# Transform and dense layers on one core: the dense layers read tokens in the order in which the transform's last stage makes them

## The chip, the cores and the metric

The kernel runs on one core of a Trainium2 chip. The metric is the device time of one execution in microseconds. The core has a matrix engine (TensorE, PE in the profile, its weight loads PEld), a vector engine (VectorE, DVE), an activation engine (ScalarE, ACT), GpSimd (POOL) and SyncE (SP), which here only issues transfers. Each takes its instructions strictly in order; they wait for each other by semaphores.

## The reference

```python
# x: (8, 3008, 256); filters: (1505, 256); w_in: (256, 2048); w_out: (2048, 256)
X = np.fft.rfft(x, axis=1)
Y = X * (filt_r + 1j * filt_i)[None]
y = np.fft.irfft(Y, n=3008, axis=1)           # 8 sequences, filtered along the tokens
h = y.reshape(24064, 256) @ w_in
g = 0.5 * h * (1.0 + erf(h / sqrt(2)))
out = g @ w_out                               # (24064, 256), float32
```

## The kernel before

Two things share TensorE: a Fourier transform with its inverse, per batch (8 batches of 3008 tokens), and two dense layers, per tile of 512 tokens (47 tiles, in the order of the tokens).

**Transform.** 3008 = 47 x 64 is split into two factors, and each direction into two stages. For batches 1 to 7 these are `s1` (L382), then a write to DRAM (`R1`) and a read back in another layout (`r1`, L413, tile `b_sb`); `s2` (L420), two matmuls and one product with the filter on VectorE (tile `p`); `s3` (L431, its second half is evacuated by `s3_out`, L448), after each group of four s2; a write to DRAM (`R2`) and a read back (`r2`, L457, tile `d_sb`); and `s4` (L465). Batch 0 goes another way, without DRAM (`c1` to `c4`), ahead of everything else.

A token of a batch has the number 32 m + w, with m from 0 to 93 and w from 0 to 31. An `s4` unit makes, for one half of the 256 channels, four values of w for all m: 376 tokens, four neighbours in every 32. Eight groups (u = 0 to 7) of two halves make a batch. They are written to `ring` (tile `y_sb`), which holds two batches with channels on the partitions, at the place of their token number:

```python
yv = self.ring[:, half, o:o + self.S].rearrange("c (m w) -> c m w", w=HB)[:, :, 4 * grp:4 * grp + 4]
```

So the first dense tile of a batch needs all sixteen units. Half 1 is evacuated by ScalarE, half 0 by VectorE (in batch 1 from group 4 on by ScalarE too).

**Dense layers.** `mm1` (L577) makes 128 of 2048 hidden values for 512 tokens, two matmuls of 512 columns, and ScalarE's gelu stores them as `g_sb`. `mm2_seven` (L643) makes the second layer of the tile before with seven instead of eight block products, so VectorE first makes sums of blocks (`sums_1` to `sums_3`, L621 to L641) and afterwards combines results (L674 to L688) in `ost`. A tile's two stores of 256 rows each, which are whole rows of the output, are issued by SyncE (L690).

**Order.** The program is written out by hand in slots, 16 per tile. A slot has what `put(slot, ...)` entered in it, in the order of the calls, then 7 matmuls of 128 columns of `mm2_seven`, then one `mm1`. Batch b is transformed while the tiles of batch b - 1 go through the dense layers; `first(b)` is the slot of the first tile with tokens of b. In the loop over batches, `s1` and `n1` are first slot and spacing of the four s1, `r1` the slot of their read-back, `s2`, `n2` and `group` first slot, spacing and length of a group of the twelve s2, `r2` the slot of the read-backs, `s4` and `n4` first slot and spacing of the sixteen s4 units. For batches 3 to 7 these sixteen stand in sixteen slots one after the other, from 17 ahead of `first(b)`.

**Buffers.** PSUM has 3 banks `h` for `mm1` (and one tile of each s1 and s3), 2 banks `o` for `mm2_seven`, and 3 banks `f` for the stages s1 to s4. `d_sb`, which holds two groups, has 3 buffers. Tile 5 (`late`) holds the last tokens of batch 0 and the first of batch 1; its `mm1` start six slots late and then go faster.

Of the kernel before, what the change touches and what calls it, by code (L numbers as in the profile page):

```python
# [20 lines left out]
HB = 32  # L21
RND = 12582912.0
TCH = 512
TURNS = 64.0


def _dram(src, off, dims):
    return dataclasses.replace(src, offset=src.offset + off, ap=[list(d) for d in dims])


class _Mix:
# [433 lines left out]
    def s4(self, b, grp, half):  # L465
        nc = self.nc
        o = b % 2 * self.S
        d = self.st[b, "d", grp // 2]
        ps = self.bank("ps_s4")
        for i in range(4):  # L470
            nc.tensor.matmul(ps[:, 94 * i:94 * i + 94],  # L471
                             lhsT=d[:, (grp % 2) * 4 + i, 128 * half:128 * half + 128],
                             rhs=self.T4a[:, 4 * grp + i], start=True, stop=True)
        yv = self.ring[:, half, o:o + self.S].rearrange("c (m w) -> c m w", w=HB)[:, :, 4 * grp:4 * grp + 4]
        pv = ps[:, 0:376].rearrange("c (i m) -> c m i", i=4)
        self._evac(yv, pv, "act" if half or b == 1 and grp > 3 else False, 1.0 / self.S)

# [75 lines left out]
    def c4(self, u, eng):  # L553

        if u == 0:

            self.ring = self.py.tile([128, 2, 2 * self.S], BF16, tag="y", name="y_sb")
        d = self.st[0, "d", u // 2]
        for half in range(2):
            ps = self.bank("ps_c4", "h" if (2 * u + half) % 5 < 3 else "o")  # L560
            for i in range(4):
                self.nc.tensor.matmul(ps[:, 94 * i:94 * i + 94],
                                      lhsT=d[:, 4 * (u % 2) + i, 128 * half:128 * half + 128],
                                      rhs=self.T4c.rearrange("p a b -> p (a b)"), start=True, stop=True)
            yv = self.ring[:, half, 0:self.S].rearrange("c (m w) -> c m w", w=HB)[:, :, 4 * u:4 * u + 4]
            self._evac(yv, ps[:, 0:376].rearrange("c (i m) -> c m i", i=4), eng[half], 1.0 / self.S)


# [22 lines left out]
    def mm2(self, t, s):  # L591
        nc = self.nc
        tile_i, q = s // 4, s % 4
        g = self.st["g", t]
        if s % 8 == 0:
            self.st["o"] = self.bank("ps_o", "o").rearrange("p (a b) -> p a b", a=2)
        ps = self.st["o"]
        for i in range(4):
            jc = 4 * q + i
            nc.tensor.matmul(ps[:, tile_i % 2, :], lhsT=g[:, jc, tile_i * 128:tile_i * 128 + 128],  # L600
                             rhs=self.w_out_sb[:, jc, :], start=(jc == 0), stop=(jc == 15))
        if s % 8 == 7:
            ost = self.po.tile([128, 2, 256], FP32, tag="ost", name="ost")
            nc.vector.tensor_copy(out=ost, in_=ps)
            r0 = t * TCH + (tile_i - 1) * 128
            nc.sync.dma_start(out=self.out[r0:r0 + 256, :].rearrange("(s p) o -> p s o", p=128), in_=ost)

    def weight_sums(self):

# [33 lines left out]
    def mm2_seven(self, t, lo, hi):  # L643

        nc, v = self.nc, self.nc.vector.tensor_tensor
        a11, a12, s2, a22 = self.quarters(t)
        w = self.w_out_sb.rearrange("p (i k) (n o) -> p k n i o", k=2, n=2)
        q = self.w_sums
        s31, s4 = self.st["s", t], self.st.get(("s4", t))
        ops = ((a11, w[:, 0, 0]), (a12, w[:, 1, 0]), (s2, q[:, 1]), (s31[:, :, 0], q[:, 2]),  # L650
               (s31[:, :, 1], q[:, 0]), (a22, q[:, 3]), (s4, w[:, 1, 1]))
        last = t == self.B * self.S // TCH - 1
        for n in range(lo, hi):
            m, sub, i = n // 16, n // 8 % 2, n % 8
# [4 lines left out]
            nc.tensor.matmul(ps[:, (m + 1) % 2, sub, :], lhsT=a[:, i, 128 * sub:128 * sub + 128], rhs=b[:, i],  # L659
                             start=i == 0, stop=i == 7)  # L660
# [12 lines left out]
            if m == 0:  # L673
                nc.vector.tensor_copy(out=t1, in_=p1)  # L674
            elif m == 2:
                v(out=c(0, 0), in0=t1, in1=p0, op=ALU.add)  # L676
                if last:
                    self.store(t, 0, 0, nc.sync)
                v(out=t1, in0=t1, in1=p1, op=ALU.add)
            elif m == 4:  # L680
                v(out=t3, in0=t1, in1=p0, op=ALU.subtract)  # L681
                v(out=c(1, 1), in0=t3, in1=p1, op=ALU.add)
                if last:
                    self.store(t, 1, 1, nc.scalar)
                v(out=t1, in0=t1, in1=p1, op=ALU.add)
            else:
                for h, tt, p in ((1, t3, p0), (0, t1, p1)):
                    v(out=c(h, 1 - h), in0=tt, in1=p, op=ALU.add)  # L688
                    r0 = t * TCH + 256 * h
                    nc.sync.dma_start(out=self.out[r0:r0 + 256, :].rearrange("(s p) o -> p s o", p=128),  # L690
                                      in_=self.st["c"][h])

    def store(self, t, h, k, eng):
        r0, k = t * TCH + 256 * h, slice(128 * k, 128 * k + 128)
        eng.dma_start(out=self.out[r0:r0 + 256, k].rearrange("(s p) o -> p s o", p=128), in_=self.st["c"][h][:, :, k])

    def finish(self, t, m, sub, ps):

        h = 6 - m
        c, tt = self.st["c"][h], self.st["t"][:, h]  # L700
        k = slice(128 * (1 - h), 128 * (1 - h) + 128)
        self.nc.vector.tensor_tensor(out=c[:, sub, k], in0=tt[:, sub], in1=ps[:, (m + 1) % 2, sub], op=ALU.add)
        if h == 1:
            if sub == 1:
                self.store(t, 1, 0, self.nc.sync)
            return
        r0 = t * TCH + 128 * sub
        (self.nc.sync if sub else self.nc.scalar).dma_start(out=self.out[r0:r0 + 128, k], in_=c[:, sub, k])


@with_exitstack
def kernel(
# [9 lines left out]
    m = _Mix(ctx, tc, x, filt_r, filt_i, moe_w_in, moe_w_out, out)  # L722
# [115 lines left out]
    def put(slot, f, *a):  # L838
        at.setdefault(slot, []).append((f, a))

    def first(b):
        return (b * S // TCH) * 16

    for b in range(1, B):
        hi = first(b)
        if b == 1:
            s1, n1, r1, s2, n2, group, r2, s4, n4 = 0, 3, 12, 27, 2.5, 12, 64, 73, 0.75
        elif b == 2:
            s1, n1, r1, s2, n2, group, r2, s4, n4 = hi - 92, 3.7, hi - 78, hi - 70, 3.4, 14, hi - 24, hi - 17, 1
        else:  # L850
            s1, n1, r1, s2, n2, group, r2, s4, n4 = hi - 94, 3.7, hi - 80, hi - 71, 3.4, 14, hi - 25, hi - 17, 1
        unit = lambda p: s2 + group * (p // 4) + int(n2 * (p % 4))
        for u in range(16):
            put(s4 + int(u * n4), m.s4, b, u // 2, u % 2)
        for c in range(4):
            put(s1 + int(c * n1), m.s1, b, c)
            put(r1 if c < 3 else unit(3) + 1, m.r1, b, c)
            put(r2 if c < 3 else s4 + int(4 * n4) + 1, m.r2, b, c)
        for p in range(12):
            put(unit(p), m.s2, b, p)  # L860
            if p % 4 == 3:
                put(unit(p) + 3, m.s3, b, p // 4)
                put(unit(p) + 4, m.s3_out, b, p // 4, 1)
        if b + 1 < B:
            for i in range(8):
                put(unit(i + 2) if b > 1 else 25, m.load_next, b, i + 2, i // 2, i % 2)

    put(0, m.table_4_rows, g)
    put(0, m.weights_4, g)
# [60 lines left out]
```

## Time and profile before

| | before |
|---|---|
| time, median of 3 runs | 751.13 us (749.76 to 751.74) |
| span of the profiled execution | 749.5 us |
| PE busy | 729.1 us (97%) |
| DVE busy | 588.9 us (79%) |
| ACT busy | 548.6 us (73%) |
| granted TensorE clock | 0.999 |
| stores by L690 and L606 | 92 transfers of 256 KB, 3.0 us to landing |

Busy shares are means over the span. The kernel has a prologue (up to about 38 us), a stretch in which batch 1 has to be made before tile 5 can use it (to about 130 us), then the same pattern per batch, and a tail after 661 us in which nothing is transformed any more.

### The profile page before, as it was taken

The page shows a single profiled execution, that of the slowest core. Times are in us where ns is not written, and L with a number is a line of the kernel's source. Part 1 is how long each engine was busy: PE and PEld are TensorE (multiplying, and loading weights), DVE is VectorE, ACT ScalarE, POOL GpSimd, SP SyncE. Part 2 cuts the span into 40 slices and gives each one's busy share as a digit, 9 for nine tenths or more (in the row PEclk, how much of TensorE's full clock was granted, in tenths as well). Part 3 has the DMA queues.
Part 4 walks back from the last instruction along what each step waited for, and adds up shares of the span by engine and source line. Part 5 has one row for each costly group of instructions (what it writes and reads, how often), then busy time and mean ns, then how long its engine had stood idle before and what let it go on. Part 6 is the DMA issues. An engine that isn't in the chain of part 4 may idle for free.

```text
span 749.5 us, 20005 instructions
## 1 busy us (share of the span) xinstructions
PE 729.1 (97%) x8286; PEld 517.9 (69%) x8420; DVE 588.9 (79%) x1053; ACT 548.6 (73%) x975; POOL 105.2 (14%) x195
## 2 busy tenths in 40 slices
PE   7999999999999999999999999999999999999998
PEld 4855666766776667666777666666677766777776
DVE  7978866897787977789777996779967798666566
ACT  6986678777786778766787667876678767777773
POOL 7979100020001200012000120002100000000000
PEclk9999999999999999999999999999999999999999
DMA  9998653565354652546625557245562432501011
GB/s 150 219 221 241 151 142 93 165 127 118 92 129 142 142 130 80 157 118 120 148 71 157 112 106 170 61 146 121 125 142 72 135 107 76 124 29 58 30 57 58
DMA packets 90187, 90.70 MB, mean 121 GB/s; under 512 B 6768, under 2 KB 76912, under 8 KB 89840
## 3 DMA queue, kind: packets, MB, share of 16 engines
q1 hardware_dynamic: 82000, 72.18, 34.9%
q0 software_dynamic: 7680, 17.04, 14.5%
q8 instruction: 66, 1.08, 0.6%
q10 hardware_dynamic: 416, 0.20, 0.1%
q14 instruction: 25, 0.20, 0.1%
HBM read 57.15 MB, written 48.23 MB: 141 GB/s over the span
## 4 chain that ended last, share of the span: by engine, by line
PE 84%; DVE 6%; DMA 4%; ACT 2%; issue 2%; POOL 0%; SPq 0%; DVEq 0%; POOLq 0%; ACTq 0%
PE ps_o L659 36%; PE ps_h L586 35%; PE ps_s L471 3%; PE ps_s L442 3%; PE ps_s L425 2%; PE ps_s L398 2%; DVE p L428 2%; DVE s_sb L628 2%; DMA R<-v_sb 2%; ACT g_sb L589 2%; DMA d_sb<-R 2%; DMA x_sb<-in_x_dram 1%; PE ps_c L533 1%; PE ps_c3t L548 1%; PE ps_c L511 0%
## 5 line engine op out<-in xcount | busy, mean ns | idle before, releaser
L589 ACT ACTIVATE g_sb<-ps_h 128x512 f16<-128x512 f32 x752 | 446.6, 599 | 181.9 <-PE ps_h L586 158.7
L586 PE MATMUL ps_h<-y_sb,w_in_sb 128*128 128x512 bf16 (+3 forms) x1470 | 417.5, 365 | 0.4
L659 PEld LDWEIGHTS <-g_sb 128*128 128x128 f16 x2944 | 193.9, 98 | 78.8 <-issue 14.8
L659 PEld LDWEIGHTS <-s_sb 128*128 128x128 f16 x2208 | 150.0, 98 | 51.6 <-issue 3.5
L586 PEld LDWEIGHTS <-w_in_sb 128*128 128x128 bf16 x1600 | 124.8, 98 | 8.0 <-issue 1.0
L659 PE MATMUL ps_o<-w_sums,g_sb 128*128 128x128 f16 x1472 | 127.3, 219 | 1.2 <-DVE g_sb L634 0.4
L659 PE MATMUL ps_o<-w_sums,s_sb 128*128 128x128 f16 x1472 | 125.8, 219 | 1.2
L628 DVE TENSOR_TENSOR s_sb<-g_sb 128x1024 f16<-128x1024 f16 x184 | 123.5, 695 | 0.3 <-ACT g_sb L589 0.3
L659 PE MATMUL ps_o<-w_out_sb,g_sb 128*128 128x128 f16 x1472 | 119.8, 219 | 2.1 <-DVE ost L688 0.4
L428 DVE TENSOR_TENSOR p<-ps_s,F 128x1024 bf16<-128x1024 f32 x84 | 102.5, 1220 | 20.3 <-PE ps_s L425 19.0
L122 POOL COPY gate<-p 1x1 bf16<-1x1 bf16 x40 | 18.7, 468 | 416.5 <-DVE p L428 416.5
L634 DVE TENSOR_TENSOR g_sb<-s_sb,g_sb 128x1024 f16<-128x1024 f16 x92 | 63.6, 691 | 1.1
L659 PE MATMUL ps_o<-w_out_sb,s_sb 128*128 128x128 f16 x736 | 63.8, 219 | 0.5
L641 DVE TENSOR_TENSOR s_sb<-g_sb 128x1024 f16<-128x1024 f16 x92 | 63.0, 684 | 0.0
L307 DVE TENSOR_SCALAR y_sb<-ps_s 128x376 bf16<-128x376 f32 x52 | 28.3, 545 | 27.7 <-PE ps_s L471 27.7
L471 PEld LDWEIGHTS <-d_sb 96*128 96x128 bf16 x448 | 31.2, 98 | 26.4 <-issue 2.6
L681 DVE TENSOR_TENSOR t_sb<-t_sb,ps_o 128x256 f32<-128x256 f32 x46 | 19.2, 416 | 38.3 <-PE ps_o L659 38.3
L305 DVE CAST a_sb<-ps_s 128x512 bf16<-128x512 f32 x57 | 36.6, 686 | 14.8 <-PE ps_s L398 14.6
L676 DVE TENSOR_TENSOR ost<-t_sb,ps_o 128x256 f32<-128x256 f32 x46 | 19.3, 419 | 33.6 <-PE ps_o L659 33.4
L471 PE MATMUL ps_s<-T4a,d_sb 96*128 96x94 bf16 x448 | 37.4, 206 | 2.7 <-DMA d_sb<-R 1.4
L688 DVE TENSOR_TENSOR ost<-t_sb,ps_o 128x256 f32<-128x256 f32 x90 | 33.6, 414 | 6.4 <-PE ps_o L659 6.4
L86 POOL DMA_DIRECT2D x_sb<-in_x_dram x64 | 32.9, 520 | 3.1 <-issue 2.9
(148 smaller groups left out, 508.7 us busy)
## 6 DMA issues: line engine op xcount, KB each, us to landing
out_dram<-ost SPq DMA_DIRECT2D x92, 256.0 KB, 3.0
x_sb<-in_x_dram POOLq DMA_DIRECT2D x64, 188.0 KB, 3.8
b_sb<-R SPq DMA_DIRECT2D x28, 384.0 KB, 4.0
R<-v_sb SPq DMA_DIRECT2D x84, 128.0 KB, 2.5
d_sb<-R SPq DMA_DIRECT2D x56, 192.0 KB, 3.9
R<-a_sb SPq DMA_DIRECT2D x54, 192.0 KB, 3.0
F<-Fd SPq DMA_DIRECT2D x4, 512.0 KB, 9.7
Fd<-F SPq DMA_DIRECT2D x8, 192.0 KB, 6.9
```

The costliest lines, as they stand in the source:

```text
L86: nc.gpsimd.dma_start(out=xt[h * o:h * o + NA, w:w + 8, :], in_=xv[h][:, w:w + 8, :])
L305: self.nc.vector.tensor_copy(out=out, in_=in_)
L307: self.nc.vector.tensor_scalar(out=out, in0=in_, scalar1=scale, scalar2=None, op0=ALU.mult)
L428: nc.vector.tensor_tensor(out=w, in0=ps.unsqueeze(1).to_broadcast([128, 2, 512]), in1=self.F[:, :, 2 * p:2 * p + 2, :].rearrange("p t a b ...
L471: nc.tensor.matmul(ps[:, 94 * i:94 * i + 94], lhsT=d[:, (grp % 2) * 4 + i, 128 * half:128 * half + 128], rhs=self.T4a[:, 4 * grp + i], sta ...
L586: nc.tensor.matmul(ps[:, o:o + n], lhsT=w[:, dc], rhs=self.ring[:, dc, off:off + n], start=(dc == 0), stop=(dc == 1))
L589: nc.scalar.activation(out=self.st["g", t][:, jc, :], in_=ps, func=AF.Gelu)
L628: self.nc.vector.tensor_tensor(out=self.st["s", t][:, i:i + 2], in0=a, in1=b, op=ALU.subtract)
L634: self.nc.vector.tensor_tensor(out=a21[:, k], in0=self.st["s", t][:, k, 0], in1=a22[:, k], op=ALU.add)
L641: self.nc.vector.tensor_tensor(out=self.st["s4", t][:, k], in0=a12[:, k], in1=s2[:, k], op=ALU.subtract)
L659: nc.tensor.matmul(ps[:, (m + 1) % 2, sub, :], lhsT=a[:, i, 128 * sub:128 * sub + 128], rhs=b[:, i], start=i == 0, stop=i == 7)
L688: v(out=c(h, 1 - h), in0=tt, in1=p, op=ALU.add)
```

## The change: token order, slots of the last stage, and the order of transfers

The ring now holds a batch group by group: 376 tokens of group 0, then group 1, and so on. A dense tile takes 512 neighbours in this order, so it needs one to three groups and not all eight. The layers act on each token alone, so the order doesn't matter to them; the stores put every row where it belongs. A store covers at most 128 rows and one group (`put_rows`); four neighbours of a group are 4 KB in a row of the output.

The units of s4 are spread. The loop at the end goes back from group 7 to group 0, and puts each unit at the latest free slot that is at least two slots ahead of the tile that first uses its group (for group 0 of batch 1 two slots into it, since that tile starts late). A slot isn't free if s1, s2, s3 or `s3_out` has it (of s1 and s3 also the neighbours); half 0 keeps clear of slots of a tile in which VectorE has sums or output steps. Between two units there is a slot at least. The read-back of the groups 2c and 2c + 1 goes to slot 12 of a tile, ahead of that tile's stores in SyncE's order, at least six slots before its first use; the first of a batch goes 7 slots after the last s2.

The other stages move a little: batch 1's s2 have 3 slots instead of 2.5 each and groups of 14 instead of 12; the s1 and s2 of later batches start 3 to 4 slots later.

```diff
-        yv = self.ring[:, half, o:o + self.S].rearrange("c (m w) -> c m w", w=HB)[:, :, 4 * grp:4 * grp + 4]
+        o += GRP * grp
+        yv = self.ring[:, half, o:o + GRP].rearrange("c (m w) -> c m w", w=4)
...
-                    r0 = t * TCH + 256 * h
-                    nc.sync.dma_start(out=self.out[r0:r0 + 256, :].rearrange("(s p) o -> p s o", p=128),
-                                      in_=self.st["c"][h])
+                    for sub in range(2):
+                        self.put_rows(t * TCH + 256 * h + 128 * sub, self.st["c"][h][:, sub], nc.sync)
+
+    def put_rows(self, r0, tile_, *engines, k=slice(0, 256)):
+
+        lo, hi = r0, r0 + 128
+        for eng in engines * 4:
+            if lo == hi:
+                return
+            b, i = divmod(lo, self.S)
+            n = min(hi - lo, GRP - i % GRP)
+            o = b * self.S + 4 * (i // GRP) + HB * (i % GRP // 4)
+            w = k.stop - k.start
+            out = _dram(self.out, o * self.D + k.start, [[HB * self.D, n // 4], [self.D, 4], [1, w]])
+            eng.dma_start(out=out, in_=tile_[lo - r0:lo - r0 + n])
+            lo += n
+        assert lo == hi
...
+    busy, after = set(), {}
     for b in range(1, B):
         hi = first(b)
         if b == 1:
-            s1, n1, r1, s2, n2, group, r2, s4, n4 = 0, 3, 12, 27, 2.5, 12, 64, 73, 0.75
+            s1, n1, r1, s2, n2, group = 0, 3, 12, 27, 3, 14
         elif b == 2:
-            s1, n1, r1, s2, n2, group, r2, s4, n4 = hi - 92, 3.7, hi - 78, hi - 70, 3.4, 14, hi - 24, hi - 17, 1
+            s1, n1, r1, s2, n2, group = hi - 88, 3.7, hi - 74, hi - 67, 3.4, 14
         else:
-            s1, n1, r1, s2, n2, group, r2, s4, n4 = hi - 94, 3.7, hi - 80, hi - 71, 3.4, 14, hi - 25, hi - 17, 1
+            s1, n1, r1, s2, n2, group = hi - 90, 3.7, hi - 76, hi - 68, 3.4, 14
...
-        for u in range(16):
-            put(s4 + int(u * n4), m.s4, b, u // 2, u % 2)
...
-            put(r2 if c < 3 else s4 + int(4 * n4) + 1, m.r2, b, c)
...
+    for b in range(1, B):
+        end = 1000000
+        for u in range(7, -1, -1):
+            due = (b * S + GRP * u) // TCH * 16
+            end = min(end, due - 2 + 4 * (u == 0 and b == 1))
+            for half in (1, 0):
+                while end in busy or half == 0 and end % 16 in (0, 1, 2, 5, 8, 12, 13, 15):
+                    end -= 1
+                put(end, m.s4, b, u, half)
+                busy.add(end)
+                end -= 2
+            if u % 2 == 0:
+                put(after[b] if u == 0 else (end - 6 - 12) // 16 * 16 + 12, m.r2, b, u // 2)
```

More of the change, by code (lines that the diff above doesn't have):

```diff
@@ L24 @@
 TURNS = 64.0
+GRP = 376
 def _dram(src, off, dims):
@@ L564, in c4 @@
                                       rhs=self.T4c.rearrange("p a b -> p (a b)"), start=True, stop=True)
-            yv = self.ring[:, half, 0:self.S].rearrange("c (m w) -> c m w", w=HB)[:, :, 4 * u:4 * u + 4]
+            yv = self.ring[:, half, GRP * u:GRP * u + GRP].rearrange("c (m w) -> c m w", w=4)
             self._evac(yv, ps[:, 0:376].rearrange("c (i m) -> c m i", i=4), eng[half], 1.0 / self.S)
@@ L604, in mm2 @@
             nc.vector.tensor_copy(out=ost, in_=ps)
-            r0 = t * TCH + (tile_i - 1) * 128
-            nc.sync.dma_start(out=self.out[r0:r0 + 256, :].rearrange("(s p) o -> p s o", p=128), in_=ost)
+            for sub in range(2):
+                self.put_rows(t * TCH + (tile_i - 1 + sub) * 128, ost[:, sub], nc.sync)
     def weight_sums(self):
@@ L688, in mm2_seven @@
                     v(out=c(h, 1 - h), in0=tt, in1=p, op=ALU.add)
-                    r0 = t * TCH + 256 * h
-                    nc.sync.dma_start(out=self.out[r0:r0 + 256, :].rearrange("(s p) o -> p s o", p=128),
-                                      in_=self.st["c"][h])
+                    for sub in range(2):
+                        self.put_rows(t * TCH + 256 * h + 128 * sub, self.st["c"][h][:, sub], nc.sync)
[12 more added lines that the diff above has]
+        assert lo == hi
     def store(self, t, h, k, eng):
-        r0, k = t * TCH + 256 * h, slice(128 * k, 128 * k + 128)
-        eng.dma_start(out=self.out[r0:r0 + 256, k].rearrange("(s p) o -> p s o", p=128), in_=self.st["c"][h][:, :, k])
+        k = slice(128 * k, 128 * k + 128)
+        for sub in range(2):
+            self.put_rows(t * TCH + 256 * h + 128 * sub, self.st["c"][h][:, sub, k], eng, k=k)
     def finish(self, t, m, sub, ps):
@@ L706, in finish @@
             return
-        r0 = t * TCH + 128 * sub
-        (self.nc.sync if sub else self.nc.scalar).dma_start(out=self.out[r0:r0 + 128, k], in_=c[:, sub, k])
+        engines = (self.nc.sync, self.nc.scalar)
+        self.put_rows(t * TCH + 128 * sub, c[:, sub, k], *(engines if sub else engines[::-1]), k=k)
 @with_exitstack
@@ L846 @@
         if b == 1:
-            s1, n1, r1, s2, n2, group, r2, s4, n4 = 0, 3, 12, 27, 2.5, 12, 64, 73, 0.75
+            s1, n1, r1, s2, n2, group = 0, 3, 12, 27, 3, 14
         elif b == 2:
-            s1, n1, r1, s2, n2, group, r2, s4, n4 = hi - 92, 3.7, hi - 78, hi - 70, 3.4, 14, hi - 24, hi - 17, 1
+            s1, n1, r1, s2, n2, group = hi - 88, 3.7, hi - 74, hi - 67, 3.4, 14
         else:
-            s1, n1, r1, s2, n2, group, r2, s4, n4 = hi - 94, 3.7, hi - 80, hi - 71, 3.4, 14, hi - 25, hi - 17, 1
+            s1, n1, r1, s2, n2, group = hi - 90, 3.7, hi - 76, hi - 68, 3.4, 14
         unit = lambda p: s2 + group * (p // 4) + int(n2 * (p % 4))
-        for u in range(16):
-            put(s4 + int(u * n4), m.s4, b, u // 2, u % 2)
         for c in range(4):
             put(s1 + int(c * n1), m.s1, b, c)
+            busy.update(range(s1 + int(c * n1) - 1, s1 + int(c * n1) + 2))
             put(r1 if c < 3 else unit(3) + 1, m.r1, b, c)
-            put(r2 if c < 3 else s4 + int(4 * n4) + 1, m.r2, b, c)
         for p in range(12):
             put(unit(p), m.s2, b, p)
+            busy.add(unit(p))
             if p % 4 == 3:
@@ L863 @@
                 put(unit(p) + 4, m.s3_out, b, p // 4, 1)
+                busy.update(range(unit(p) + 2, unit(p) + 6))
+        after[b] = unit(11) + 7
         if b + 1 < B:
```

## The prediction

> **What bounds the kernel now.** I read the busy times and the chain that ended last on the page, then the timeline of TensorE in steady state, then the waits, then the places where TensorE stood still. The page first, one line of its busy part and one of its chain:
>
> ```profile
> PE 729.1 (97%) x8286; PEld 517.9 (69%) x8420; DVE 588.9 (79%) x1053; ACT 548.6 (73%) x975; POOL 105.2 (14%) x195
> ...
> PE 84%; DVE 6%; DMA 4%; ACT 2%; issue 2%; POOL 0%; SPq 0%; DVEq 0%; POOLq 0%; ACTq 0%
> ```
>
> TensorE is busy for 97% and carries 84% of the chain. That alone doesn't say it runs at its peak, so I look at how densely its rows follow each other. The columns of the timeline are start, duration, engine, line, operation. Eight rows inside and just after a burst of the last transform stage (s4, L471):
>
> ```profile
> 191.64 0.59 PE L586 MATMUL ps_h<-y_sb,w_in_sb 128*128 128x512 bf16 x2
> 192.07 0.34 PE L471 MATMUL ps_s<-T4a,d_sb 96*128 96x94 bf16 x4
> 192.25 0.55 PE L659 MATMUL ps_o<-w_out_sb,g_sb 128*128 128x128 f16 x7
> 192.64 0.59 PE L586 MATMUL ps_h<-y_sb,w_in_sb 128*128 128x512 bf16 x2
> ...
> 204.66 0.59 PE L586 MATMUL ps_h<-y_sb,w_in_sb 128*128 128x512 bf16 x2
> 205.09 0.55 PE L659 MATMUL ps_o<-w_out_sb,s_sb 128*128 128x128 f16 x7
> 205.48 0.59 PE L586 MATMUL ps_h<-y_sb,w_in_sb 128*128 128x512 bf16 x2
> ```
>
> The reader is to see the period: 205.48 - 204.66 = 0.82 us for a plain slot, 192.64 - 191.64 = 1.00 us for a slot with an s4 unit. So a unit costs 0.18 us, and the burst of sixteen that the change dissolves has no bubble in it: nothing is to be had by thinning it out as such. Gains can only come from places where TensorE waits. The waits view names them (who waited for whom: us in total, times, longest):
>
> ```profile
> PEld L659 <- DVE ost L688: 1.5, 5, 0.6
> ...
> PE ps_s L471 <- DMA d_sb<-R: 1.4, 3, 0.8
> ...
> PE ps_s L442 <- ACT v_sb L303: 1.0, 1, 1.0
> ...
> PE ps_s L442 <- DVE p L428: 0.8, 1, 0.8
> PEld L659 <- DVE g_sb L634: 0.8, 2, 0.5
> ```
>
> Together 5.5 us of 749.5. The largest single ones lie in the first dense tiles, where batch 1 must be transformed in a hurry. One is this, from the chain in that window (start, duration, what):
>
> ```profile
> 81.88 0.61 PE ps_s L442 x8
> 82.53 1.09 ACT v_sb L303 x2
> 83.66 0.62 PE ps_s L442 x7
> ```
>
> TensorE stops in the middle of an s3 (sixteen matmuls), until ScalarE has emptied two banks of the same s3; the timeline has 1.02 us of idle time there, and 1.3 us between two starts beyond the usual. The other is the round trip through DRAM before batch 1's s4, again from the chain:
>
> ```profile
> 95.06 1.06 PE ps_s L442 x16
> ...
> 97.58 1.09 ACT v_sb L303 x2
> ...
> 99.19 2.41 DMA R<-v_sb
> ...
> 101.65 0.96 SPq L462
> ...
> 102.66 3.71 DMA d_sb<-R
> ...
> 106.51 0.51 PE ps_s L471 x8
> ```
>
> From the end of s3 (96.12) to the landing of d_sb (106.37) are 10.25 us.
>
> **What the Trainium skill says.** "Perfetto Trace Analysis", section "Identifying the Most-Contended Engine", warns that matmul busy time isn't a measure of closeness to the limit, because matmuls are pipelined; the trace agrees (rows of 0.59 us start 0.43 apart), hence the period above. "DMA: Bandwidth & Descriptors", section "Anatomy of one DMA — SWDGE (gpsimd) path", puts a fixed cost of about 2.0 us on a transfer, mostly completion; it speaks of another issuing path, yet here a 256 KB store lands after 3.0 us and a 128 KB v_sb write after 2.5, so halving a transfer saves little. The same page, section "Issuing engines are not separate DMA queues", says that all queues share the 16 engines; no run so far shows whether more stores on SyncE delay the loads. "SBUF — State Buffer", section "SBUF: two separate sides", lets VectorE and GpSimd exclude each other on a shared port pair; the trace fits it: s_sb sums take 1.24 us at 63.86 while tables are made on GpSimd, 0.69 on the mean.
>
> **The change part by part.** TensorE's instructions are the same in number and kind (8420 matmuls in both programs); only their order differs. So each part is a wait removed or added.
>
> 1. *Second s3 of batch 1.* In the program before, the fourth bank of this s3 is the bank of its own second (the wait is for the evacuation emitted after it). With s2 spaced 3 instead of 2.5 slots and 14 per group, the new program gives it the bank of an s2 tile. The products before it, 1.14 us each, fit with the sums into their 3 slots, so no new wait: **-1.3 us**.
>
> 2. *First s3 of batch 1* (waits of 0.8 for p and 0.5 for g_sb, 1.7 us of lost starts). VectorE works without a gap from 59.1 to 70.97 there. s3 moves two slots back, so it no longer waits, but the second-layer matmuls need the sum of slot 34, now finished at 70.97 less the fourth product (1.14) = 69.8, while TensorE would arrive at 67.8. A wait of 2.0 us with the s3 (1.0 us) still to come, against 1.7 with it done and 1.14 more of VectorE behind: at slot 39 both stand at about 72.4. **0**.
>
> 3. *Batch 1's d_sb.* Before, 12 slots lie between s3 and s4 (61 to 73): 12 x 0.82 = 9.9, and 10.25 + 0.14 - 9.9 = 0.5 is waited. After, they are 11 (67 to 78): 9.05, so the wait is 1.2. The read-back now is two transfers instead of eight, but the first two led the queue before too. **+0.6 us**.
>
> 4. *d_sb of later batches.* Waits of 0.83 and 0.33 us before. The reads are put 16 slots ahead of s4 at the start of a batch and at least 8 later on; 8 x 0.82 = 6.6 us against 3.9 to land, and nothing that waits long stands ahead of them on SyncE, since they go before that tile's stores. **-1.1 us**.
>
> 5. *s4 among s2 and s3.* The stretch of s2 was full on VectorE: 40 slots hold 2.5 tiles x (8 sums x 0.60 + 8 output steps x 0.37) = 19.4, 12 products x 1.14 = 13.7, 6 casts x 0.6 = 3.6, together 36.7 us beside TensorE's 40 x 0.82 + 12 x 0.22 + 3 x 1.0 = 38.4. Now three s4 evacuations of 0.5 us join, while their six units give TensorE 1.1 us more. On the mean it fits; locally it doesn't. In two batches s4 of group 6 stands two slots ahead of an s3 (243 and 245, 339 and 341) that takes over its bank. VectorE enters that tile about 0.9 us late (from slot 10: evacuation 0.5, two products 2.3, three output steps 1.1, three sums 1.8, and 0.7 idle until the first inputs are there, 6.4 in all, against TensorE's 6 x 0.82 + 0.18 + 2 x 0.22 = 5.5). It then has two output steps 0.74, sums 1.8, a product 1.14, a copy 0.35 and the evacuation 0.5 to do: 0.9 + 4.5 = 5.4 us, where TensorE arrives after 5 x 0.82 + 0.22 + 0.18 + 0.5 = 5.0. **+0.7 us** for both with 0.35 each. The five waits for L688 stay: an s4 put at slot 11 adds 0.5 to VectorE's queue, but TensorE gets 0.18 + 0.22 later to the bank; one new s2 at slot 15 in batch 2 adds **+0.2**.
>
> 6. *b_sb.* s2 begins 11 slots after the last s1 instead of 12. Before, an s1 at 309.39 was read back from an issue at 314.92, so with 4.0 us in use at 318.9, 9.5 us later. After, 11 x 0.82 + 0.63 and 0.18 to 0.54 for s4 give 9.8 to 10.2. But stores stand ahead of the last R write on SyncE: five or six at 0.42 us (two took 1.02), and they share the engines. Between 0 and 0.5 per batch; I take **+0.3** in all.
>
> 7. *Stores.* SyncE issues 487 transfers instead of 333, 154 x 0.42 = 65 us more on a queue that mostly waits: hidden, as bytes and row length stay. The buffers come back 9 slots after; 6 to 7 us of issue and landing fit in 7.4. At the end two issues more on SyncE and one on ScalarE: **+0.2**.
>
> ScalarE: gelu runs at 0.51 us back to back (seven in 3.56) against 0.82 per slot, so 0.48 for a y_sb is absorbed; the tile-5 rush has the same 0.8 us excess before and after. The evacuation at the latest slot (14) has two slots until the first layer reads it. No wait.
>
> Sum: -1.3 - 1.1 + 0.6 + 0.7 + 0.2 + 0.3 + 0.2 = -0.4; 751.1 - 0.4 = **750.7 us**.
>
> **The rivals.** *It goes faster.* The removed waits count and the added ones don't come: d_sb lands sooner because only two reads are under way, banks are free in time, and spreading also takes VectorE's backlog at tile ends (1.5 us). Then -1.3 - 1.1 - 1.5 = -3.9: 747.2. For it: TensorE's waits fall exactly where the change loosens spacing. Against: VectorE's 79% and the full s2 stretch.
> *It goes slower.* Transfers become the wait: stores in front of R writes make b_sb late by 0.6 us in six batches (3.6), and one s3 in every batch, not in two, waits 0.35 for an s4 bank (2.1). With parts 1, 3, 4, 7 and the 0.2 of part 5 that is -1.3 + 0.6 - 1.1 + 0.2 + 0.2 + 3.6 + 2.1 = +4.3, so 755.4. For it: slack for b_sb was only about 1 us. Against: the queues move 121 GB/s, half of what they show elsewhere (241).
>
> **How the numbers follow.** Forecast (no measurable change, within 2.25 us of 751.1) 0.46; faster 0.31, since every wait named above could vanish but none that is added is certain; slower 0.23. Unknown are part 6 (0 to 2.5), part 3 (0 to 1.2), part 5 (0 to 4). The faster rival with the tail's 0.2 and part 3's wait (0.5) gone too gives 746.5; the slower rival 755.4. Range 746.5 to 755.5.
>
> **What would show it.** Right: s4 units one by one at 0.18 us with no wait for d_sb but the first, whose wait is about 1.2; no stop inside the second s3; the page's TensorE busy time as before. Wrong: waits of L425 for b_sb over 1 us in total, s3 waiting for y_sb evacuations by more than 1.5 us in total, or first-layer matmuls (L588 in the new numbering) waiting for y_sb, which I exclude.

## The result, and the profile after

| | before | after |
|---|---|---|
| time, median | 750.8 us (749.76 to 751.74, 4 runs) | 759.33 us (758.58 to 760.27, 4 runs) |
| ratio to before | | 1.0115 (95%: 1.0096 to 1.0133) |
| span of the profiled execution | 749.5 us | 757.7 us |
| stores on SyncE up to 735 us: number, issue in total, mean | 90, 41.2 us, 0.46 us | 235, 163.3 us, 0.70 us |

The change makes the kernel 8.5 us slower; the forecast was 750.7 us and a range up to 755.5. The page of the profile after, the same two lines as before:

```profile
PE 730.3 (96%) x8286; PEld 517.5 (68%) x8420; DVE 588.9 (78%) x1053; ACT 548.1 (72%) x975; POOL 103.3 (14%) x195
...
PE 81%; DMA 7%; DVE 5%; issue 3%; ACT 3%; POOL 1%; SPq 1%; DVEq 0%; POOLq 0%; ACTq 0%
```

The busy times of the engines are those of before (TensorE 730.3 against 729.1 us), so no engine has more to do. The chain has changed: TensorE's share falls from 84 to 81%, that of DMA rises from 4 to 7%. The waits view names the transfer (who waited for whom: us in total, times, longest):

```profile
PEld L661 <- DVE g_sb L636: 5.5, 8, 1.7
...
PE ps_s L426 <- DMA b_sb<-R: 5.3, 7, 1.7
...
PE ps_o L661 <- DVE g_sb L636: 3.1, 6, 1.4
...
PE ps_s L472 <- DMA d_sb<-R: 1.4, 1, 1.4
```

Of the five lines shown of before, those for `ost` (1.5 us) and for the second s3's own evacuation (1.0 us) are gone but for 0.2 us at `ost`, `d_sb` is down to a single wait, and all seven batches wait for `b_sb` (before, batch 1 alone lost 0.5 us there). A row for the weight loads and one for the matmuls can describe the same stop, so I don't add these. For a sum I took TensorE's rows in order of time and subtracted from each step between two starts the usual step of its kind; what is left at a stop is lost time:

| TensorE's lost time, us | before | after | difference |
|---|---|---|---|
| s2 waits for `b_sb` | 0.49 | 6.48 (0.68, 0.89, 0.33, 0.89, 1.88, 0.60, 1.21) | +6.0 |
| second layer waits for the sum `g_sb` in a tile's slot 4, tiles 13, 19, 25 and 31 | 0 | 2.07 (4 stops) | +2.1 |
| the same in tile 5 | 0 | 0.53 | +0.5 |
| from the last matmul to the end | 3.14 | 4.87 | +1.7 |
| s3 waits for the bank of an s4 | 0 | 0.70 (272.48 and 364.74 us) | +0.7 |
| first s3 of batch 1 and the sums beside it | 1.69 | 1.84 | +0.2 |
| s4 waits for `d_sb` | 1.91 | 1.55 | -0.4 |
| second layer waits for `ost` | 1.50 | 0.23 | -1.3 |
| second s3 of batch 1 | 1.34 | 0 | -1.3 |

These make +8.2 us, the difference of the two spans. Three quarters of it is `b_sb`, nearly all in batches 2 to 7; batch 1, which has no stores in its way, had the wait before too. Here is how it comes about in batch 4. First SyncE's timeline of before (start, time from the first issue to the end of the last, line, what, how many):

```profile
303.29 8.72 SPq L411 DMA_DIRECT2D R<-a_sb  x6
312.69 1.02 SPq L690 DMA_DIRECT2D out_dram<-ost  x2
314.92 1.29 SPq L417 DMA_DIRECT2D b_sb<-R  x3
```

All R1 writes are issued, then two stores, then the read-back. The same view after:

```profile
310.84 0.82 SPq L412 DMA_DIRECT2D R<-a_sb  x2
312.33 4.68 SPq L705 DMA_DIRECT2D out_dram<-ost  x6
317.13 1.07 SPq L412 DMA_DIRECT2D R<-a_sb  x2
320.75 1.30 SPq L418 DMA_DIRECT2D b_sb<-R  x3
```

Six stores hold the queue for 4.7 us, and the last two R1 writes, whose data had been there since 314.7 (the last evacuation), wait behind them until 317.13. In the chain of batch 5, the longest case, each link can be seen (start, duration, what):

```profile
405.68 0.47 PE ps_s L399 x4
406.15 1.28 DVE a_sb L306 x2
...
408.10 0.85 SPq L705
...
408.99 0.59 SPq L705
...
409.69 0.52 SPq L412
...
410.27 3.00 DMA R<-a_sb
...
413.32 3.78 DMA b_sb<-R
417.10 0.04 issue
417.14 0.38 PE ps_s L426 x2
```

The evacuation ends at 407.4; the write goes out at 409.7, after the last stores; write and read-back take 6.8 us more, and s2 starts at 417.14, 1.88 us too late. In the kernel before, the same leg, from the issue of the batch's last write to the landing of the first read-back, took 7.1 us: the transfers aren't slower, they only start later.

### The profile page after: what moved, and what is told of

It is laid out like the page before. It is cut to its first block, busy times and chain, and to the rows that moved or that the text cites. A ratio compares the mean times of both kernels' runs of the same rounds, so it can differ in the third digit from the quotient of the medians.

```text
span 757.7 us, 20236 instructions
## 1 busy us (share of the span) xinstructions
PE 730.3 (96%) x8286; PEld 517.5 (68%) x8420; DVE 588.9 (78%) x1053; ACT 548.1 (72%) x975; POOL 103.3 (14%) x195
## 4 chain that ended last, share of the span: by engine, by line
PE 81%; DMA 7%; DVE 5%; issue 3%; ACT 3%; POOL 1%; SPq 1%; DVEq 0%; POOLq 0%; ACTq 0%
PE ps_o L661 35%; PE ps_h L588 34%; DMA b_sb<-R 3%; PE ps_s L443 3%; PE ps_s L426 3%; PE ps_s L472 3%; DMA R<-a_sb 2%; ACT g_sb L591 2%; PE ps_s L399 2%; DVE s_sb L630 1%; DVE g_sb L636 1%; DMA x_sb<-in_x_dram 1%; DMA F<-in_filt_i_dram 1%; PE ps_c L535 1%; DVE p L429 1%
## 5 line engine op out<-in xcount | busy, mean ns | idle before, releaser
L661 PEld LDWEIGHTS <-g_sb 128*128 128x128 f16 x2944 | 196.1, 98 | 85.2 <-issue 10.5
L661 PEld LDWEIGHTS <-s_sb 128*128 128x128 f16 x2208 | 147.2, 98 | 47.9 <-issue 8.2
L429 DVE TENSOR_TENSOR p<-ps_s,F 128x1024 bf16<-128x1024 f32 x84 | 102.4, 1219 | 17.9 <-PE ps_s L426 17.9
L123 POOL COPY gate<-p 1x1 bf16<-1x1 bf16 x40 | 16.1, 404 | 425.3 <-DVE p L429 425.3
L636 DVE TENSOR_TENSOR g_sb<-s_sb,g_sb 128x1024 f16<-128x1024 f16 x92 | 63.6, 691 | 1.2
L472 PEld LDWEIGHTS <-d_sb 96*128 96x128 bf16 x448 | 31.8, 98 | 26.2 <-DMA d_sb<-R 1.8
L472 PE MATMUL ps_s<-T4a,d_sb 96*128 96x94 bf16 x448 | 38.1, 206 | 2.0 <-DMA d_sb<-R 1.4
L690 DVE TENSOR_TENSOR ost<-t_sb,ps_o 128x256 f32<-128x256 f32 x90 | 33.6, 414 | 6.9 <-PE ps_o L661 6.7
L426 PE MATMUL ps_s<-b_sb,T2p 128*128 128x256 bf16 x168 | 32.1, 273 | 6.2 <-DMA b_sb<-R 5.3
L426 PEld LDWEIGHTS <-T2p 128*128 128x128 bf16 x168 | 16.2, 98 | 25.9 <-issue 5.4
```

The source lines that it names most:

```text
L426: nc.tensor.matmul(ps[:, 256 * i:256 * i + 256], lhsT=self.T2p[:, k].rearrange("p a b c d -> p (a b c d)"), rhs=self.st[b, "b", k // 6][:, ...
L429: nc.vector.tensor_tensor(out=w, in0=ps.unsqueeze(1).to_broadcast([128, 2, 512]), in1=self.F[:, :, 2 * p:2 * p + 2, :].rearrange("p t a b ...
L472: nc.tensor.matmul(ps[:, 94 * i:94 * i + 94], lhsT=d[:, (grp % 2) * 4 + i, 128 * half:128 * half + 128], rhs=self.T4a[:, 4 * grp + i], sta ...
L636: self.nc.vector.tensor_tensor(out=a21[:, k], in0=self.st["s", t][:, k, 0], in1=a22[:, k], op=ALU.add)
```

## The experiments

Each kernel of the experiments was timed in five rounds beside the kernel before (medians of 750.7 to 750.9 us). Batch 4 in the second table is one example; the columns are us from the start of the last s1's last matmul.

| kernel | time, us | ratio to before (95%) |
|---|---|---|
| after | 759.33 | 1.0115 (1.0096 to 1.0133) |
| a_s1early: s1 4 slots earlier | 753.69 | 1.0035 (1.0023 to 1.0048) |
| a_whole: two stores per tile | 751.19 | 1.0001 (0.9993 to 1.0010) |
| a_half: four, neighbouring rows | 750.63 | 0.9995 (0.9987 to 1.0004) |
| a_uncut: four, scattered | 751.72 | 1.0012 (1.0004 to 1.0020) |
| a_cut: five or six, neighbouring rows | 750.77 | 1.0000 (0.9992 to 1.0008) |
| b_scatter: before with the new stores | 772.11 | 1.0279 (1.0265 to 1.0293) |
| a_s1s2: a_s1early, s2 1 slot later | 750.90 | 1.0006 (0.9998 to 1.0014) |
| a_s1s2b1: and batch 1 as before | 751.57 | 1.0017 (1.0009 to 1.0025) |
| a_s1s2tail: a_s1s2, last stores in part on GpSimd | 755.94 | 1.0070 (1.0057 to 1.0082) |
| a_best1: a_s1s2, fewer pieces at the end | 750.80 | 0.9999 (0.9991 to 1.0008) |
| a_last: a_s1s2, last batch as before | 750.38 | 0.9992 (0.9985 to 0.9998) |

| kernel | mean issue of a store | a tile's stores take | last R1 write | first `b_sb` read |
|---|---|---|---|---|
| before | 0.46 | 1.0 (2) | 1.9 | 5.3 |
| a_half | 0.47 | 2.0 (4) | 1.9 | 5.8 |
| a_uncut | 0.65 | 2.5 (4) | 2.9 | 6.3 |
| a_cut | 0.46 | 3.8 (6) | 3.5 | 6.5 |
| after | 0.70 | 4.7 (6) | 4.5 | 7.5 |

### s1 earlier

For batches 3 to 7 (batch 2 likewise, from `hi - 88` and `hi - 74` to `hi - 92` and `hi - 78`):

```diff
-            s1, n1, r1, s2, n2, group = hi - 90, 3.7, hi - 76, hi - 68, 3.4, 14
+            s1, n1, r1, s2, n2, group = hi - 94, 3.7, hi - 80, hi - 68, 3.4, 14
```

> The changed kernel with the four s1 of batches 3 to 7 starting 4 slots earlier (hi - 94, batch 2 hi - 92, as before the change) and their read-backs too (hi - 80, hi - 78), s2 left where it is. Theory Q (SyncE's queue: the last two R1 writes stand behind a tile's five or six stores, 0.70 us of issue each): the last writes are issued 1.6 us after the last s1 instead of 2.6 to 3.9, and s2 comes 15 instead of 11 slots after it, so the b_sb waits of batches 2 to 7 (5.8 us) go and about 753.5 us is left. Theory M (the spread s4 units themselves cost the time, on VectorE and TensorE; the b_sb waits only take up idle time that would come anyway): the waits go, but the time stays within 2 us of 759.

It took 753.69 us, and there is no wait for `b_sb` left in batches 2 to 7. SyncE's timeline, again batch 4:

```profile
309.31 0.82 SPq L412 DMA_DIRECT2D R<-a_sb  x2
310.80 4.91 SPq L705 DMA_DIRECT2D out_dram<-ost  x6
315.81 1.50 SPq L418 DMA_DIRECT2D b_sb<-R  x3
```

The writes now go ahead of the stores, and only the read-backs stand behind them. The `b_sb` waits were real and not time that would have been idle anyway: theory Q is right and M falls. The same stops at L636, at the bank of s4 and at the end stay as they were (2.07, 0.72 and a tail of 4.96 us). This run moves the writes and also gives 4 slots more of room, so it alone can't tell the queue from slow transfers; the next ones do.

### Fewer stores, or stores of another form

In a_whole the stores are those of before (L690 of the old program); in a_half `put_rows` writes 128 neighbouring rows:

```diff
-            n = min(hi - lo, GRP - i % GRP)
...
-            eng.dma_start(out=out, in_=tile_[lo - r0:lo - r0 + n])
+            n = hi - lo
+            eng.dma_start(out=self.out[lo:hi, k], in_=tile_)
```

> The changed kernel with the stores of before the change: two of 256 rows per tile, in the order in which the rows come out, so it leaves out putting the rows in their places. Theory Q: two issues of 0.46 us stand ahead of the last R1 writes instead of six of 0.70, so the b_sb waits of batches 2 to 7 fall from 5.8 to under 1 us, and the tail is 1.7 us shorter: 752. Theory C (the bytes of the stores share the 16 DMA engines with R1 write and read-back, the place in the queue doesn't matter): the b_sb waits stay over 4 us, only the tail gets shorter, 757.5.

> The changed kernel with stores of 128 neighbouring rows in the order in which they come out, four per tile: it leaves out putting the rows in their places. Tells the number of transfers from their form. If an issue costs the same whatever its form (0.46 us as before the change, theory Q1), four take 1.8 us and the b_sb waits of batches 2 to 7 are 1 to 2 us: 753.5. If the number of issues sets it at 0.70 us each (Q2), four take 2.8 us and the waits are 2.5 to 3.5 us: 756. Theory C: waits over 4 us, 758.

Both are as fast as the kernel before (751.19 and 750.63 us), with s4 spread, the same slots and the same bytes stored. So neither the spread units nor the bytes cost the 8.5 us (M and C fall); the form and number of the stores do. The spread units aren't free, though: in a_half's trace the four stops at L636 (2.07 us) and the two at the bank of an s4 (0.7 us) are still there, and the waits that the change takes away (second s3 1.3, `d_sb` 1.5, `ost` 1.3) pay for them. a_half was faster than Q1 expected: its four issues fit entirely into the time that the last evacuation takes anyway:

```profile
308.54 2.01 SPq L701 DMA_DIRECT2D out_dram<-ost  x4
311.00 1.69 SPq L412 DMA_DIRECT2D R<-a_sb  x2
```

The stores begin 0.9 us before the last s1's last matmul and the R1 writes have their data 1.6 us after it. That gives 2.5 us in which the stores cost nothing. Behind it, s2 had about 1 us of slack in batches 3 to 7, from the landing of the first read-back to its start (0.2 us in batch 2).

Number and form are told apart by a_uncut (scattered four and four, never cut; the destination is another set of rows) and a_cut (cut where groups end, neighbouring rows). The edit of a_cut:

```diff
-            out = _dram(self.out, o * self.D + k.start, [[HB * self.D, n // 4], [self.D, 4], [1, w]])
-            eng.dma_start(out=out, in_=tile_[lo - r0:lo - r0 + n])
+            eng.dma_start(out=self.out[lo:lo + n, k], in_=tile_[lo - r0:lo - r0 + n])
```

> The changed kernel with four stores of 128 rows per tile, each scattered four and four rows like those of the change, but never cut where a group ends; it leaves out putting the rows in their places. Together with a_half (four stores, neighbouring rows, 750.6 us) and the changed kernel (five or six stores, scattered and cut, 759.3 us) it tells the scattering from the cutting. In the changed kernel's trace a scattered store of 128 rows takes 0.60 us to issue, a cut piece 0.59 to 0.92. If these issue times set the delay, four take 2.4 us against 1.9 in a_half and some 5 in the changed kernel: the R1 writes come at most 0.6 us later than in a_half, b_sb waits of 0 to 2 us in all, 751 to 753. If scattering as such is what delays (landing, the engines' share), the waits stay over 4 us: 756 to 758.

> The changed kernel with its stores cut where groups end, as in the change, but each piece written to neighbouring rows in the order in which they come out; it leaves out putting the rows in their places. The fourth corner: a_half is neither cut nor scattered (750.6), a_uncut scattered only (751.7), the changed kernel both (759.3). In the changed kernel pieces of 16 or 32 runs of four rows took 0.59 to 0.60 us to issue and all others 0.68 to 0.92, whatever their size. Theory K (the division counts: what doesn't divide by 16 costs more): pieces whose number of rows is a multiple of 16 (112, 96, 80, 64, 48, 32, 16) take 0.45 us like the uncut ones, all others (120, 104, 88, 72, 56, 40, 24, 8) 0.15 us more or above; six stores then take 3.0 to 3.6 us, b_sb waits of 1 to 3 us in all, 752.5 to 755. Theory N (only the number and the scattering count): all pieces take 0.45 us, six take 2.7 us, waits under 1 us, 751 to 752.5.

751.72 and 750.77 us: each alone costs next to nothing. Scattering alone raises an issue from 0.47 to 0.65 us, cutting alone raises the number from four to five or six. Only together they fill the queue for 4.7 us, 2.2 more than were free, and eat the slack of 1 us as well. The cost is a threshold, not a sum. Theory K falls: in a_cut pieces of 8, 24, 40 and 104 rows took 0.35 to 0.37 us on the mean, no more than pieces of 16 and 64 rows (0.61, with one issue of 1.6 us among eight, and 0.54). So why a scattered piece of a number of runs other than 16 or 32 takes 0.68 to 0.92 us stays open; the runs show only that it does.

The Trainium skill, "Perfetto Trace Analysis", section "What "DMA-bound" means", says that the profiled window of an issuing engine is the making of descriptors (the orders to the DMA engines), not the moving of data, and that a kernel is bound there when that engine's track is solid with issues. The trace agrees with the first: the stores' issues took 41 us before and 163 after, for the same bytes. The second isn't so here: all of SyncE's issues together fill 305 of 757.7 us (40%), and TensorE waits all the same, because a write with a deadline stands behind six of them. "DMA: Bandwidth & Descriptors", section "Anatomy of one DMA — SWDGE (gpsimd) path", calls that making small and variable for the other issuing path; here, from SyncE, it went from 0.35 to 0.92 us with the form of the transfer.

### The new stores in the kernel before

```diff
-            nc.sync.dma_start(out=self.out[r0:r0 + 256, :].rearrange("(s p) o -> p s o", p=128), in_=self.st["c"][h])
+            for sub in range(2):
+                self.put_rows(r0 + 128 * sub, self.st["c"][h][:, sub], nc.sync)
```

> The kernel before with the stores of the changed one (up to 128 rows of one group, scattered four and four; since its tokens stand in another order, it puts rows in other places than it should). Everything else as before. Theory Q: here the R1 writes stand ahead of the stores, but the b_sb reads behind them; they are issued about 2 us later, and the slack of 1.0 to 1.5 us is used up, so b_sb waits of 0.5 to 1 us in batches 2 to 7 (3 to 6 us) and a tail longer by 1.7 us: 756 to 758.5. Theory M: the stores cost only their tail, 752.5.

772.11 us, 21 us slower, far beyond what any theory said. The direction of Q was right, but it had left out the other read-back. SyncE before the s4 of one batch:

```profile
368.28 4.69 SPq L704 DMA_DIRECT2D out_dram<-ost  x6
373.42 2.61 SPq L456 DMA_DIRECT2D R<-v_sb  x4
377.85 3.35 SPq L463 DMA_DIRECT2D d_sb<-R  x6
```

Its waits view has 11.5 us for `d_sb` at L472 in six stops (the longest 3.8 us), besides 5.3 us for `b_sb`. The R2 writes stand behind the stores there, and all sixteen units of s4 stand behind them. That isn't all. After the two longest stops (3.8 us until 109.0 and 2.1 us until 382.4) the trace shows TensorE's granted clock at half for 3.4 us, from 110.5 and from 383.6; the same pair of matmuls then takes nearly twice as long (start, duration):

```profile
382.93 0.59 PE L587 MATMUL ps_h<-y_sb,w_in_sb 128*128 128x512 bf16 x2
...
384.24 1.06 PE L587 MATMUL ps_h<-y_sb,w_in_sb 128*128 128x512 bf16 x2
```

No stop of 1.6 us or less in this trace was followed by such a stretch. At half the clock 3.4 us are worth 1.7, so the two cost some 3.4 us by estimate. Lost time by TensorE's starts was 12.5 us for `d_sb` and 6.2 for `b_sb`, against 1.9 and 0.5 in the kernel before; with 1.7 us more tail and the 3.4 these make the 21 us. So the parts of the change go together: the new stores alone are much worse, and with the new slots ahead of s4 the damage stays with `b_sb`.

### The other stops

The third s2 of batches 3 to 7 falls on slot 2 of a tile after the change; in four of the five the second layer stops. VectorE's timeline there (after, tile 13):

```profile
238.14 0.68 DVE L630 TENSOR_TENSOR s_sb<-g_sb 128x1024 f16<-128x1024 f16 x1
238.74 1.22 DVE L429 TENSOR_TENSOR p<-ps_s,F 128x1024 bf16<-128x1024 f32 x1
239.88 0.68 DVE L636 TENSOR_TENSOR g_sb<-s_sb,g_sb 128x1024 f16<-128x1024 f16 x1
```

The product (L429) comes ahead of the sum (L636) that the second layer waits for. One slot later it would come behind (the edit is shown against a_s1early; batch 2 stays at `hi - 67`):

```diff
-            s1, n1, r1, s2, n2, group = hi - 94, 3.7, hi - 80, hi - 68, 3.4, 14
+            s1, n1, r1, s2, n2, group = hi - 94, 3.7, hi - 80, hi - 67, 3.4, 14
```

> The changed kernel with s1 4 slots earlier (as in the run a_s1early) and s2 of batches 3 to 7 one slot later (hi - 67 instead of hi - 68). In the changed kernel the third s2 of a batch falls on slot 2 of a tile, where its product (1.14 us on VectorE) stands ahead of the sum that the second layer needs at slot 4; at hi - 67 it falls on slot 3, behind that sum, as in batch 2, which shows no such wait. If the position of the product is the cause, the four stops of 0.52 us (g_sb, L636) go and the time is 751.6 us. If VectorE is simply too full there (theory M), a stop of the same size comes back a few slots later and the time stays at 753.7.

750.90 us, 2.8 below a_s1early. All four stops are gone, and with them the two at the bank of an s4 (2.07 + 0.72 = 2.8). That the two figures are the same is chance: the waits for `ost` come back with the new slot (five of 0.23 us against one), and about 0.9 us less is lost at the first s3 and `d_sb` of batch 1, which the edit doesn't touch. So the place of the product ahead of the sum makes the four stops (theory M had a stop of the same size come back; what comes back is shorter), and the slot of s2 is worth some 1.9 us by these traces. VectorE works in the other order now:

```profile
235.66 0.69 DVE L636 TENSOR_TENSOR g_sb<-s_sb,g_sb 128x1024 f16<-128x1024 f16 x1
236.26 0.42 DVE L676 COPY t_sb<-ps_o 128x256 f32<-128x256 f32 x1
236.60 1.22 DVE L429 TENSOR_TENSOR p<-ps_s,F 128x1024 bf16<-128x1024 f32 x1
```

Batch 1 as before the change (`27, 2.5, 12` in place of `27, 3, 14`):

> As a_s1s2, with the s2 of batch 1 as before the change (2.5 slots each, groups of 12). Tests the first three steps of the forecast: the second s3 of batch 1 gets its own bank back and stops for 1.3 us; the third s3 is 6 slots earlier, so its R2 writes come ahead of a tile's stores, and the wait for batch 1's d_sb (1.5 us lost) goes; the first s3 waits as before (0 to 0.2 us of difference). The steps together: within 0.6 us of a_s1s2. If the second s3 costs nothing, 1.5 us faster; if d_sb stays late, 1.3 us slower.

751.57 us, 0.7 above a_s1s2. The second s3 stops again (1.34 us, the same two pieces of the chain as before the change), the first s3 and the sum beside it lose 0.5 us more, and there is no wait for batch 1's `d_sb` any more (1.01 us in a_s1s2). The expected trade is there, at nearly the expected size. That the R2 writes' place behind the stores makes this wait agrees with a_half, where the slots are those of the change and the wait is 0.41 us instead of 1.55.

The tail. In a_s1s2tail the stores of the upper half of the last tile but one, and one of the last tile, are issued by GpSimd:

```diff
-                        self.put_rows(t * TCH + 256 * h + 128 * sub, self.st["c"][h][:, sub], nc.sync)
+                        self.put_rows(t * TCH + 256 * h + 128 * sub, self.st["c"][h][:, sub],
+                                      nc.gpsimd if h and t == self.B * self.S // TCH - 2 else nc.sync)
...
-                self.store(t, 1, 0, self.nc.sync)
+                self.store(t, 1, 0, self.nc.gpsimd)
```

> As a_s1s2, with the last stores taken off SyncE in part: those of the upper half of the tile before the last, and the last but one store of the last tile, are issued by GpSimd. In the changed kernel SyncE issues eleven stores without a pause in the last 8.2 us and ends 1.4 us after VectorE's last result. If that queue makes the tail longer (1.7 us more from the last result to the end than before the change), the time is 1.0 to 1.7 us below a_s1s2. If it is the landing of the last store itself, it is the same.

755.94 us, 5.0 slower. TensorE's last matmul ends at 743.3, SyncE's last issue at 744.4, ScalarE's at 746.0, yet the span ends at 752.5. GpSimd's own rows:

```profile
737.09 1.87 POOL L706 DMA_DIRECT2D out_dram<-ost  x3 [201.97 <-DVE ost L690]
743.27 1.10 POOL L706 DMA_DIRECT2D out_dram<-ost  x2 [4.31 <-DVE ost L720]
```

They end at 744.4 too, but a drain on GpSimd's sequencer (an instruction at the end of the program) lasts from 743.75 to 751.71, and the other engines' last instructions come after it. Nor was SyncE the queue that ended last: in a_s1s2 its last issue ended at 745.6, ScalarE's at 746.6.

a_best1 stores the last tile's upper half in whole rows, one part by SyncE and one by ScalarE, and swaps the engines of the last pieces:

```diff
-                if last:
-                    self.store(t, 1, 1, nc.scalar)
...
-                self.store(t, 1, 0, self.nc.sync)
+                for s, eng in enumerate((self.nc.sync, self.nc.scalar)):
+                    self.put_rows(t * TCH + 256 + 128 * s, c[:, s], eng)
...
-        self.put_rows(t * TCH + 128 * sub, c[:, sub, k], *(engines if sub else engines[::-1]), k=k)
+        self.put_rows(t * TCH + 128 * sub, c[:, sub, k], *engines[::-1], k=k)
```

> As a_s1s2, with a shorter queue at the end: the upper half of the last tile is stored in whole rows, one part by SyncE and one by ScalarE, instead of in two column halves, and of the very last part ScalarE takes the short piece and SyncE the long one. In a_s1s2 the last result is there at 744.2 and the span ends at 748.75 (4.5 us, 2.8 before the change), after a store on ScalarE that was issued until 746.6. If the number of pieces on the two queues makes the tail, it ends 0.8 to 1.2 us earlier: 749.9 us, below both kernels. If the landing of any scattered piece makes it, it is the same as a_s1s2.

750.80 us; the tail is 4.57 us instead of 4.86, and the time is the same. ScalarE's last piece, of eight rows, alone took 1.19 us to issue. The number of pieces in the last microseconds is therefore not the whole cause. a_last keeps the last batch in the order of the tokens, and its stores whole, two of 256 rows per tile (that part isn't shown):

```diff
+        if b == self.B - 1:
+            yv = self.ring[:, half, o:o + self.S].rearrange("c (m w) -> c m w", w=HB)[:, :, 4 * grp:4 * grp + 4]
...
+        if b == B - 1:
+            s1, r1, s2 = hi - 97, hi - 83, hi - 71
...
+    for u in range(16):
+        put(first(B - 1) - 17 + u, m.s4, B - 1, u // 2, u % 2)
...
-    for b in range(1, B):
+    for b in range(1, B - 1):
```

> As a_s1s2, but the last batch keeps the order of the tokens as before the change: its sixteen s4 stand one after the other ahead of its first tile, its s1 and s2 start at hi - 97 and hi - 71, its stores are whole and uncut, two of 256 rows per tile, the last ones as before. Batches 1 to 6 are those of a_s1s2. If the cut stores of the last two tiles make the tail, it takes 3.1 instead of 4.9 us after TensorE's last matmul, and the time is 749.1 us, 1.7 below a_s1s2 and the kernel before. The risk is batch 7: its b_sb and d_sb now stand behind cut stores of batch 6, with distances of 14 and 12 slots; a wait of 1 us at either takes most of it back (750.5).

750.38 us, half a microsecond below the kernel before (0.9992, interval 0.9985 to 0.9998). The tail is 3.16 us again. The forms of the stores give the tails an order: 3.14 us for whole stores (before, a_whole), 3.23 neighbouring halves, 3.58 cut, 3.90 scattered, 4.9 both. Of the 1.7 us, batch 7 took 0.79 back by a wait for `d_sb`, as feared. This is the best version of the study, and it gains hardly anything.

## Why the prediction was wrong

The mechanism was in the forecast, and most parts went the way they were said to; two terms were far too small, both for the price of an issue, and one wait was missed. Without these two, the forecast was -0.9 us and the trace has +0.5; that they are so near is partly luck, since the `ost` waits that went unforeseen (-1.3) make up for much of the wait that was missed (+2.1).

**Part 6 (`b_sb`), forecast +0.3, measured +6.0: the failed step.** It had the right place: s2 one slot nearer to the last s1, and five or six stores ahead of the last R1 write. But it took 0.42 us for each store, from the rows of before, which are whole stores. A scattered store takes 0.60, a cut and scattered piece 0.68 to 0.92 (0.59 with 16 runs). With 0.42, six take 2.5 us, which the runs show to be just what is free, so next to no delay. With the measured 4.7 us for six the last write of batch 4 goes out 2.6 us later than before. In a_half, a_uncut and a_cut, with the same slots and with queues of 2.0 to 3.8 us, at most 0.4 us of stops for `b_sb` are left, so this term makes the 6 us. The prediction gave part 6 at most 2.5 us, and 3.6 in the slower rival, with no row of that form to go by, since before shows none; so the range ended at 755.5. The stated sign of a wrong forecast, over 1 us at L426, is what came.

**Part 7 (tail), forecast +0.2, measured +1.7.** The price of an issue again, and ScalarE's more than SyncE's. The last issues of before, and after it (start, time to the end of the last issue):

```profile
746.71 0.41 SPq L708 DMA_DIRECT2D out_dram<-ost  x1
```

```profile
746.33 8.21 SPq L705 DMA_DIRECT2D out_dram<-ost  x11
751.98 3.56 ACTq L705 DMA_DIRECT2D out_dram<-ost  x4
```

Before, the last issue ended 0.8 us after TensorE's last matmul. After, SyncE's eleven end 1.7 us and ScalarE's four 2.7 us after it; the last of the four, 120 rows of half a row each, alone took 1.44 us. All of SyncE's issues grew by 141 us and not by 65; where no write or read-back stands behind them, and apart from the end, the table of lost time shows no stop that they cause.

**Part 5, forecast +0.7 and +0.2.** The two stops at the bank of an s4 came where they were foreseen, 0.35 us each. The waits for `ost` did not stay (1.50 to 0.23 us); with s2 one slot later, in a_s1s2, they are back. The prediction weighed where s2 and s4 stand for the banks only, and not for the order on VectorE: the third s2, now at slot 2, stands ahead of a sum, 2.07 us. The 0.53 us in tile 5 are as long where batch 1's `d_sb` isn't late (a_s1s2b1, a_uncut), so that isn't their cause; it stays open.

**Part 1, forecast -1.3:** -1.34, and a_s1s2b1 brings it back. **Part 2, 0:** +0.15. **Part 3, +0.6:** +0.97. Its own terms give a wait of 1.3 us (10.25 + 0.14 - 9.05) and not 1.2, so +0.8; that the R2 writes stand behind the stores too would be the rest. **Part 4, -1.1:** -1.33.

The slower rival named the true mechanism, stores in front of R1 writes, but with 3.6 us for it, and it was given 23%. Its other term, an s3 in every batch that waits for the bank of an s4 (2.1 us), didn't come: there were two, as in the forecast.

## What to carry to other kernels

A transfer's price on the queue that issues it belongs to its form: read the duration of that form, or take a range for it, before putting more of them ahead of something that is waited for. On a queue in strict order, extra issues are free up to the moment when a write or read-back with a deadline stands behind them, and then they cost time, here up to 1.9 us per batch; list what is queued behind them, stage by stage, with the time it has to spare. Moving a stage by a slot can turn the order of two instructions on a full engine, so look at both neighbours of the new slot.

## What the runs showed of the hardware that was not expected

- A scattered store of 128 rows (32 runs of four rows, 1 KB each) takes SyncE 0.60 to 0.65 us, one of 128 neighbouring rows 0.47, one of 256 rows in two blocks 0.46; a scattered piece of eight rows (two runs) 0.70. The bytes hardly matter.
- Whole stores of 256 KB land 3.0 us after issue, halves 2.0 (a_half), scattered halves 2.2 (a_uncut). The prediction had it that halving saves little; it saved a third.
- Stores issued by GpSimd at the very end kept the program alive for 7.3 us after the last of their issues, in a drain of 8.0 us (a_s1s2tail); without them the span ended 2.1 us after the last issue (a_s1s2).
- After stops of 3.8 and 2.1 us TensorE's granted clock was half for 3.4 us each time (b_scatter), starting 1.5 and 1.2 us after the matmuls had begun again; after the stops of up to 1.9 us in the changed kernel it stayed whole.
